# Four column groups in the second feed-forward product, one store, and w1 in three transfers of 112, 8 and 8 partitions

## The chip, the cores and the metric

The kernel runs on one core of a Trainium2 chip. The metric is the device time of one execution in microseconds (us); the kernel before takes 87.88 us, the median of three runs from 87.72 to 87.97. The profile shows one execution whose span, from the first to the last recorded instruction, is 86.1 us. Times inside the kernel are counted from the start of that span.

## What is computed

One decode step of a transformer block for four sequences (B = 4, one token each, width D = 512). A vector `c` is turned into six modulation vectors; then come attention over the last 1024 cached positions and a feed-forward layer with ReLU, each behind a layer norm that is scaled and shifted, and each added back through a gate:

```python
mod = (_silu(c) @ w_mod).reshape(c.shape[0], 6, 1, -1)
sa, ca, ga, sb, cb, gb = (mod[:, i] for i in range(6))
h = _layernorm(x) * (1 + ca) + sa
x = x + ga * attention(h, k_cache, v_cache, wq, wo)   # 32 heads, 8 key heads
h = _layernorm(x) * (1 + cb) + sb
x = x + gb * (relu(h @ w1) @ w2)                       # w1: 512 x 1792, w2: 1792 x 512
```

(The six slices are written as a loop here; the reference copies them one by one.) All inputs are bf16. Every weight and every cache entry is used once, so some 32 MB are read for very little arithmetic.

## The kernel before

All loads are issued by the SyncE queue (SP), in the order in which they are wanted: two key tiles, w_mod, wq in four parts, six more key tiles, eight value tiles, wo in four parts of 1 MB (`WO_CHUNKS`, L112 to 114), w1 as one transfer of 128 partitions (L119) and w2 in three transfers of 768, 768 and 256 KB (`W2_CHUNKS`, L123 to 125). The order of instructions on the other engines is the order of the program; each engine waits where its operands are not there yet.

Activations are kept transposed: features on the partitions, the four sequences along the free axis (`xT`, `xs2`, `h2T`). Three matmuls want the four sequences as the *stationary* operand: the gate `gb` (`gb_ps`, L227), the residual brought back to rows (`x12_ps`, L381) and the second feed-forward product (`z_ps`, L400). For these, `siluT32`, `xs2` and `uT32` are tiles with 32 columns (CG = 32), zero but for columns 0 to 3. A stationary operand of 32 columns fills a quarter of TensorE's columns, a column group. The kernel uses NH = 2 of the four groups: group 0 makes output columns 0 to 255 and writes to PSUM partitions 0 to 31, group 1 makes columns 256 to 511 and writes to partitions 32 to 63. So z_ps has 64 partitions, of which 0 to 3 and 32 to 35 carry results.

The end of the kernel, step by step: the last part of wo ends the attention product `y_ps` (L367: 128 matmuls, 32 for each part); VectorE adds the residual (L372, L373); `layernorm_T` (L242 to L261) takes two matmuls, six small VectorE operations and two ScalarE ones to make `h2T`; `ffn1` (L393) makes the hidden units in groups that follow W2_CHUNKS, 14 blocks of 128, each from four matmuls, and VectorE applies the ReLU (L395) into `uT32`; `ffn2` (L400) multiplies each block by its rows of w2 in two matmuls of 256 columns; VectorE multiplies by the gate (L410) and adds the residual (L412); two stores, one from SyncE and one from ScalarE, write the two halves of the rows (L414, L415).

```python
for (m0, m1) in U_GROUPS:
    ffn1(m0, m1)
for (m0, m1) in U_GROUPS:
    ffn2(m0, m1)
```

So TensorE does all of ffn1, then all of ffn2, and each group of ffn2 waits for its own transfer of w2.

Of the kernel before, what the change touches and what calls it, by code (L numbers as in the profile page):

```python
# [9 lines left out]
ALU = mybir.AluOpType  # L10
# [7 lines left out]
def kernel(  # L18
# [14 lines left out]
    nc = tc.nc  # L33
    P = 128
    B, Sq, D = A_x.shape
# [9 lines left out]
    CG = 32  # L45
# [7 lines left out]
    NI = W // KC  # L53
    RB = KC
    KAHEAD = 2
    NH = 2
    DH2 = D // NH

    ctx.enter_context(tc.manual_schedule(engines={
        mybir.EngineType.PE, mybir.EngineType.Activation, mybir.EngineType.DVE, mybir.EngineType.Pool}))  # L60
# [28 lines left out]
    wmod_sb = wts.tile([P, DT, 6 * D], bf16, tag="med", name="wmod_sb")  # L89
# [9 lines left out]
    for h in range(Hkv):  # L99
        vt_ = kvpool.tile([P, NI, Dh], bf16, tag="kv", name=f"v{h}")  # L100
        nc.sync.dma_start(
            out=vt_[:].rearrange("p j d -> p (j d)"),
            in_=A_v_cache[:, h, S - W:, :].rearrange("b (p j) d -> p b (j d)", j=NI),
# [5 lines left out]
    wo_sb = wts.tile([P, Hkv, NL, D], bf16, tag="big", name="wo_sb")  # L109
    wo_src = A_wo.rearrange("(h p l) n -> p h (l n)", h=Hkv, l=NL)  # L110
    wo_dst = wo_sb[:].rearrange("p h l n -> p h (l n)")
    WO_CHUNKS = [(0, 2), (2, 4), (4, 6), (6, 8)]  # L112
    for (h0, h1) in WO_CHUNKS:
        nc.sync.dma_start(out=wo_dst[:, h0:h1, :], in_=wo_src[:, h0:h1, :])

    w12 = wts.tile([P, DT * Dff + FT * D], bf16, tag="med", name="w12")
    w1_sb = w12[:, 0:DT * Dff].rearrange("p (t n) -> p t n", t=DT)
    w2_sb = w12[:, DT * Dff:DT * Dff + FT * D].rearrange("p (m n) -> p m n", m=FT)
    nc.sync.dma_start(out=w1_sb, in_=B_w1.rearrange("(t p) n -> p t n", p=P))  # L119
    FT2 = FT // 2  # L120
    w2_src = B_w2.rearrange("(m2 q e) n -> q m2 (e n)", q=P, e=2)
    w2_dst = w12[:, DT * Dff:DT * Dff + FT * D].rearrange("p (m2 en) -> p m2 en", m2=FT2)
    W2_CHUNKS = [(0, 3), (3, 6), (6, FT2)]  # L123
    for (m0, m1) in W2_CHUNKS:
        nc.sync.dma_start(out=w2_dst[:, m0:m1, :], in_=w2_src[:, m0:m1, :])  # L125

# [10 lines left out]
    siluT32 = const.tile([P, DT, CG], bf16, name="siluT32")  # L137
    nc.gpsimd.memset(siluT32[:], 0.0)
    ident_f = const.tile([P, P], f32, name="ident_f")
# [14 lines left out]
    uT32 = const.tile([P, FT, CG], bf16, name="uT32")  # L154
    nc.gpsimd.memset(uT32[:], 0.0)
    xs2 = const.tile([P, DT, CG], f32, name="xs2")
# [6 lines left out]
    cT = tp0[:, :, 0:B]  # L163
# [4 lines left out]
    f_c = work.tile([P, DT, B], f32, name="f_c")  # L168
# [2 lines left out]
    nc.vector.tensor_scalar_add(out=t_c[:], in0=t_c[:], scalar1=1.0)  # L171
    nc.vector.reciprocal(out=t_c[:], in_=t_c[:])
    nc.vector.tensor_tensor(out=f_c[:], in0=f_c[:], in1=t_c[:], op=ALU.mult)
    nc.vector.tensor_tensor(out=siluT32[:, :, 0:B], in0=cT, in1=f_c[:], op=ALU.mult)
    xT = work.tile([P, DT, B], f32, name="xT")
    nc.vector.tensor_copy(out=xT[:], in_=tp0[:, :, B:2 * B])

# [39 lines left out]
    mT = psA.tile([P, 5, DT, B], f32, tag="t", name="mT")  # L217
    for k in range(5):
        for m in range(DT):
            n0 = k * D + m * P  # L220
            for t in range(DT):
                nc.tensor.matmul(out=mT[:, k, m, :], lhsT=wmod_sb[:, t, n0:n0 + P], rhs=siluT32[:, t, 0:B],  # L222
                                 start=(t == 0), stop=(t == DT - 1))
    gb_ps = psA.tile([NH * CG, DH2], f32, tag="t", name="gb_ps")
    for t in range(DT):
        for nh in range(NH):
            nc.tensor.matmul(out=gb_ps[nh * CG:(nh + 1) * CG, :], lhsT=siluT32[:, t, :],  # L227
                             rhs=wmod_sb[:, t, 5 * D + nh * DH2:5 * D + (nh + 1) * DH2],
                             start=(t == 0), stop=(t == DT - 1), tile_position=(0, nh * CG))
    modT = work.tile([P, 5, DT, B], f32, name="modT")  # L230
    nc.vector.tensor_copy(out=modT[:], in_=mT[:])
    gb2 = work.tile([NH * CG, DH2], f32, name="gb2")
    nc.scalar.copy(out=gb2[:], in_=gb_ps[:])
# [35 lines left out]
    for t in range(DT):  # L269
        for hq in range(Hq):  # L270
            nc.tensor.matmul(out=qT_v[:, hq, :], lhsT=wq_sb[:, t, hq * Dh:(hq + 1) * Dh], rhs=hT[:, t, :],  # L271
                             start=(t == 0 and hq == 0), stop=(t == DT - 1 and hq == Hq - 1))
    for par in range(2):
        dst = qpad_s[:, :, par * NHW * CG:(par + 1) * NHW * CG].rearrange("p b (h c) -> p b h c", h=NHW)
        nc.vector.tensor_copy(  # L275
            out=dst[:, :, :, 16 * par:16 * par + rep],
            in_=qT_ps[:, par].rearrange("p h r b -> p b h r"))
# [35 lines left out]
    for iq in range(NQ):  # L313
        ws = slice(iq * WQ, (iq + 1) * WQ)
        nc.scalar.activation(out=e_sb[:, ws].rearrange("q (u k e) -> q u k e", k=KC, e=2),  # L315
                             in_=sc_ps[:, ws].rearrange("q (u e k) -> q u k e", e=2, k=KC), func=ACT.Exp,
                             bias=nb[:], scale=scale, accum_out=den4[:, iq:iq + 1])
    for iq in range(NQ):
        ws = slice(iq * WQ // 2, (iq + 1) * WQ // 2)
        nc.vector.tensor_tensor(out=p_w[:, ws, :], in0=e_w[:, ws].unsqueeze(2).to_broadcast([P, WQ // 2, B]),  # L320
                                in1=mi4[:].unsqueeze(1).to_broadcast([P, WQ // 2, B]), op=ALU.bitwise_and)
# [21 lines left out]
    for h in range(VEARLY, Hkv):  # L343
        pv(h, 0, NI, last=(h == Hkv - 1))
        if h == VEARLY:
# [6 lines left out]
                            in0=oT_ps[:].rearrange("p h a b r -> p (h a b r)"), in1=rb[:], op=ALU.mult)  # L352

    o4_ps = psA.tile([P, NL, NHW, 2, B], f32, tag="t", name="o4_ps")
    for l in range(NL):
        for r in range(rep):
            nc.tensor.matmul(out=o4_ps[r * RB:(r + 1) * RB, l], lhsT=ident_k3[:, l, :], rhs=oT_sb[:, :, :, :, r],
                             start=True, stop=True, tile_position=(0, r * RB))
# [5 lines left out]
    for h in range(Hkv):  # L364
        for l in range(NL):
            for m in range(DT):
                nc.tensor.matmul(out=y_ps[:, m, :], lhsT=wo_sb[:, h, l, m * P:(m + 1) * P], rhs=o4[:, l, h % NHW, h // NHW, :],  # L367
                                 start=(h == 0 and l == 0 and m == 0),
                                 stop=(h == Hkv - 1 and l == NL - 1 and m == DT - 1))
    yT = work.tile([P, DT, B], f32, name="yT")  # L370
    x1T = xs2[:, :, 0:B]
    nc.vector.tensor_tensor(out=yT[:], in0=y_ps[:], in1=ga, op=ALU.mult)  # L372
    nc.vector.tensor_tensor(out=x1T, in0=yT[:], in1=xT[:], op=ALU.add)  # L373

# [2 lines left out]

    x12_ps = psA.tile([NH * CG, DH2], f32, tag="t", name="x12_ps")
    for t in range(DT):
        nh, tl = t // 2, t % 2  # L380
        nc.tensor.matmul(out=x12_ps[nh * CG:(nh + 1) * CG, tl * P:(tl + 1) * P], lhsT=xs2[:, t, :], rhs=ident_f[:],  # L381
                         start=True, stop=True, tile_position=(0, nh * CG))


    w1_cols = [w1_sb[:, t, :].rearrange("p (m2 q e) -> p m2 e q", q=P, e=2) for t in range(DT)]
    z_ps = psA.tile([NH * CG, DH2], f32, tag="t", name="z_ps")
    U_GROUPS = [(2 * a, 2 * b_) for (a, b_) in W2_CHUNKS]

    def ffn1(m0, m1):
        u_ps = psA.tile([P, m1 - m0, B], f32, tag="t", name=f"u_ps_{m0}")  # L390
        for m in range(m0, m1):
            for t in range(DT):
                nc.tensor.matmul(out=u_ps[:, m - m0, :], lhsT=w1_cols[t][:, m // 2, m % 2, :], rhs=h2T[:, t, :],  # L393
                                 start=(t == 0), stop=(t == DT - 1))
        nc.vector.tensor_scalar_max(out=uT32[:, m0:m1, 0:B], in0=u_ps[:], scalar1=0.0)  # L395

    def ffn2(m0, m1):
        for m in range(m0, m1):
            for nh in range(NH):
                nc.tensor.matmul(out=z_ps[nh * CG:(nh + 1) * CG, :], lhsT=uT32[:, m, :],  # L400
                                 rhs=w2_sb[:, m, nh * DH2:(nh + 1) * DH2],
                                 start=(m == 0), stop=(m == FT - 1), tile_position=(0, nh * CG))

    for (m0, m1) in U_GROUPS:
        ffn1(m0, m1)
# [4 lines left out]
    nc.vector.tensor_tensor(out=zg[:], in0=z_ps[:], in1=gb2[:], op=ALU.mult)  # L410
    res = work.tile([NH * CG, DH2], bf16, name="res")
    nc.vector.tensor_tensor(out=res[:], in0=zg[:], in1=x12_ps[:], op=ALU.add)  # L412
    out_r = out.rearrange("b o d -> (b o) d")
    nc.sync.dma_start(out=out_r[:, 0:DH2], in_=res[0:B, :])  # L414
    nc.scalar.dma_start(out=out_r[:, DH2:D], in_=res[CG:CG + B, :])  # L415


# [28 lines left out]
```

## Time and profile before

| what | value |
|---|---|
| time, median of 3 | 87.88 us |
| span of the profiled execution | 86.1 us |
| TensorE matmul busy | 53.5 us, 62% of the span |
| VectorE, ScalarE busy | 23.7 us (28%), 22.8 us (26%) |
| read from memory | 31.99 MB, 373 GB/s mean over the span |
| transfers on the load queue | 90.8% of 16 engines' span |
| granted TensorE clock, mean | 0.713 |
| ffn1 matmuls (L393) | 56, from 77.5 us |
| ffn2 matmuls (L400) | 28, from 79.1 us, 418 ns each |
| the two stores issued | 83.64 and 83.65 us |

The share of busy time of the engines is a mean over stages. What sets the end is read from the chain that ended last: that is 69% transfers, 15% the SyncE queue's issuing and 10% TensorE. A matmul's duration is from its start to its end in a pipeline, so several can overlap, and the busy time of a group is less than the count times the duration.

### The profile page before, as it was taken

The page shows a single profiled execution, that of the slowest core. Times are in us where ns is not written, and L with a number is a line of the kernel's source. Part 1 is how long each engine was busy: PE and PEld are TensorE (multiplying, and loading weights), DVE is VectorE, ACT ScalarE, POOL GpSimd, SP SyncE. Part 2 cuts the span into 40 slices and gives each one's busy share as a digit, 9 for nine tenths or more (in the row PEclk, how much of TensorE's full clock was granted, in tenths as well). Part 3 has the DMA queues.
Part 4 walks back from the last instruction along what each step waited for, and adds up shares of the span by engine and source line. Part 5 has one row for each costly group of instructions (what it writes and reads, how often), then busy time and mean ns, then how long its engine had stood idle before and what let it go on. Part 6 is the DMA issues. An engine that isn't in the chain of part 4 may idle for free.

```text
span 86.1 us, 2373 instructions
## 1 busy us (share of the span) xinstructions
PE 53.5 (62%) x1074; PEld 45.0 (52%) x1074; DVE 23.7 (28%) x63; ACT 22.8 (26%) x35; POOL 3.5 (4%) x17
## 2 busy tenths in 40 slices
PE   0029920595393899999996099947354443379840
PEld 0029920574382379777881099937244443259510
DVE  0043470023200105765556695000020000432030
ACT  2314750001200026887773674010000000020000
POOL 6900000000000000000000000000000000000000
PEclk9999999755555557999999965975555555555555
DMA  0799999999999999999999999999999999999200
GB/s 2 329 415 412 414 425 425 428 426 415 426 426 423 415 423 419 415 411 423 426 407 419 419 426 426 430 407 411 411 402 411 413 396 410 399 389 353 101 0 2
DMA packets 6009, 32.14 MB, mean 373 GB/s; under 512 B 480, under 2 KB 496, under 8 KB 3440
## 3 DMA queue, kind: packets, MB, share of 16 engines
q1 hardware_dynamic: 5976, 31.99, 90.8%
q8 instruction: 8, 0.13, 0.6%
q10 hardware_dynamic: 24, 0.01, 0.1%
q14 instruction: 1, 0.01, 0.0%
HBM read 31.99 MB, written 0.00 MB: 372 GB/s over the span
## 4 chain that ended last, share of the span: by engine, by line
DMA 69%; SPq 15%; PE 10%; DVE 1%; issue 1%; DVEq 0%
DMA wq_sb<-in_A_wq_dram 27%; DMA v<-in_A_v_cache_dram 23%; DMA w<-in_B_w_dram 19%; SPq L119 5%; SPq L125 5%; PE ktp L187 5%; PE z_ps L400 2%; PE sc_ps L199 2%; SPq L94 2%; SPq L81 1%; PE qT_ps L271 1%; SPq L90 1%; DVE zg L410 0%; DVE res L412 0%; DVE qpad L275 0%
## 5 line engine op out<-in xcount | busy, mean ns | idle before, releaser
L192 ACT COPY kT<-ktp 128x1024 bf16<-128x1024 bf16 x16 | 15.5, 1015 | 15.2 <-PE ktp L187 14.1
L187 PEld LDWEIGHTS <-k 128*128 128x128 bf16 x256 | 17.1, 109 | 3.9 <-DMA k<-in_A_k_cache_dram 2.2
L187 PE MATMUL ktp<-ident_k,k 128*128 128x128 bf16 x256 | 18.1, 239 | 1.3 <-DMA k<-in_A_k_cache_dram 1.3
L190 DVE COPY kT<-ktp 128x1024 bf16<-128x1024 bf16 x16 | 11.1, 692 | 11.7 <-PE ktp L187 11.4
L309 PE MATMUL oT_ps<-pT,v 128*128 128x16 bf16 x256 | 7.5, 172 | 3.2 <-issue 1.7
L309 PEld LDWEIGHTS <-v 128*128 128x128 bf16 x256 | 7.2, 101 | 3.5 <-issue 1.8
L367 PE MATMUL y_ps<-o,wo_sb 128*128 128x4 bf16 x128 | 4.1, 167 | 5.3 <-DMA wo_sb<-in_A_wo_dram 5.3
L367 PEld LDWEIGHTS <-wo_sb 128*128 128x128 bf16 x128 | 3.7, 104 | 5.7 <-DMA wo_sb<-in_A_wo_dram 5.7
L255 ACT ACTIVATE lnv_ln<-var_ln,eps_t 128x4 f32<-128x4 f32 x2 | 0.6, 298 | 21.5 <-DVE var_ln L253 21.5
L271 PE MATMUL qT_ps<-hT,wq_sb 128*128 128x4 bf16 x128 | 3.9, 166 | 3.3 <-DMA wq_sb<-in_A_wq_dram 1.7
L199 PE MATMUL sc_ps<-kT,qpad 128*32 128x512 bf16 x64 | 5.6, 445 | 0.4 <-DVE qpad L275 0.4
L271 PEld LDWEIGHTS <-wq_sb 128*128 128x128 bf16 x128 | 3.7, 104 | 3.5 <-DMA wq_sb<-in_A_wq_dram 1.9
L222 PE MATMUL mT<-siluT,wmod_sb 128*128 128x4 bf16 x80 | 2.3, 166 | 4.7 <-DMA wmod_sb<-in_w_mod_dram 4.7
L326 PE MATMUL pT_ps<-ident_bf,p_rep 128*128 128x128 bf16 x32 | 3.1, 278 | 2.9 <-DVE p_rep L320 2.9
L222 PEld LDWEIGHTS <-wmod_sb 128*128 128x128 bf16 x80 | 2.2, 104 | 4.9 <-DMA wmod_sb<-in_w_mod_dram 4.9
L326 PEld LDWEIGHTS <-p_rep 128*128 128x128 bf16 x32 | 2.7, 127 | 3.4 <-DVE p_rep L320 3.4
L400 PE MATMUL z_ps<-w,uT 128*32 128x256 bf16 x28 | 3.4, 415 | 0.3 <-DMA w<-in_B_w_dram 0.3
L162 PE MATMUL tp<-ident_bf,cx_sb 8*128 8x8 bf16 x4 | 0.2, 163 | 4.6 <-DMA cx_sb<-in_A_x_dram 4.6
L351 DVE TENSOR_TENSOR oT_sb<-oT_ps,rb 128x128 bf16<-128x128 f32 x1 | 0.3, 292 | 9.4 <-PE oT_ps L309 9.4
L320 DVE TENSOR_TENSOR p_rep<-e_sb,mi 128x512 int32<-128x512 int32 x4 | 2.5, 688 | 0.7 <-ACT e_sb L315 0.7
L372 DVE TENSOR_TENSOR yT<-y_ps,modT 128x16 f32<-128x16 f32 x1 | 0.2, 174 | 9.1 <-PE y_ps L367 9.1
L400 PEld LDWEIGHTS <-uT 128*32 128x32 bf16 x28 | 2.0, 137 | 1.1 <-issue 0.6
(76 smaller groups left out, 35.3 us busy)
## 6 DMA issues: line engine op xcount, KB each, us to landing
k<-in_A_k_cache_dram SPq DMA_DIRECT2D x8, 1024.0 KB, 21.2
v<-in_A_v_cache_dram SPq DMA_DIRECT2D x8, 1024.0 KB, 19.8
wq_sb<-in_A_wq_dram SPq DMA_DIRECT2D x4, 1024.0 KB, 17.5
wo_sb<-in_A_wo_dram SPq DMA_DIRECT2D x4, 1024.0 KB, 20.1
wmod_sb<-in_w_mod_dram SPq DMA_DIRECT2D x1, 3072.0 KB, 14.0
w<-in_B_w_dram SPq DMA_DIRECT2D x1, 1792.0 KB, 22.2
w<-in_B_w_dram SPq DMA_DIRECT2D x2, 768.0 KB, 18.1
w<-in_B_w_dram SPq DMA_DIRECT2D x1, 256.0 KB, 13.7
```

The costliest lines, as they stand in the source:

```text
L119: nc.sync.dma_start(out=w1_sb, in_=B_w1.rearrange("(t p) n -> p t n", p=P))
L125: nc.sync.dma_start(out=w2_dst[:, m0:m1, :], in_=w2_src[:, m0:m1, :])
L187: nc.tensor.transpose(out=tp[:, ii, :], in_=k_tiles[gi][:, iq * IQ + ii, :], identity=ident_k)
L190: nc.vector.tensor_copy(out=dst, in_=tp[:])
L192: nc.scalar.copy(out=dst, in_=tp[:])
L199: nc.tensor.matmul(out=sc_ps[hw * CG:(hw + 1) * CG, half * HALF:(half + 1) * HALF], lhsT=qpad[:, b, par, hw, :], rhs=kT[:, half * (NI // 2 ...
L222: nc.tensor.matmul(out=mT[:, k, m, :], lhsT=wmod_sb[:, t, n0:n0 + P], rhs=siluT32[:, t, 0:B], start=(t == 0), stop=(t == DT - 1))
L271: nc.tensor.matmul(out=qT_v[:, hq, :], lhsT=wq_sb[:, t, hq * Dh:(hq + 1) * Dh], rhs=hT[:, t, :], start=(t == 0 and hq == 0), stop=(t == DT ...
L309: nc.tensor.matmul(out=oT_ps[:, hw, par].rearrange("p b r -> p (b r)"), lhsT=v_tiles[h][:, i, :], rhs=pT[:, i, c0:c0 + B * rep], start=(fi ...
L326: nc.tensor.transpose(out=tp[:, ii, :], in_=p_rep[:, i // 2, :, i % 2], identity=ident_bf[:])
L367: nc.tensor.matmul(out=y_ps[:, m, :], lhsT=wo_sb[:, h, l, m * P:(m + 1) * P], rhs=o4[:, l, h % NHW, h // NHW, :], start=(h == 0 and l == 0 ...
L400: nc.tensor.matmul(out=z_ps[nh * CG:(nh + 1) * CG, :], lhsT=uT32[:, m, :], rhs=w2_sb[:, m, nh * DH2:(nh + 1) * DH2], start=(m == 0), stop= ...
```

## The change

NH goes from 2 to 4, so the three products with a 32-column stationary operand use all four column groups, with 128 output columns for each. Within a group of 32 the four sequences now stand in every eighth column (BS = CG // B = 8) rather than in the first four. As 4 groups x 4 sequences then are 16 partitions spaced evenly by 8, one strided read of `res` holds the whole result, and one store replaces two. The writers and readers of siluT32, xs2 and uT32 take the stride.

The loads are cut differently. The last part of wo becomes two of 512 KB; w2's second transfer becomes two (512 and 256 KB), which also makes four groups of ffn1 and ffn2 out of three; w1 is loaded as partitions 0 to 111, 112 to 119 and 120 to 127. This gives the DMA engines uneven shares of w1, while the same bytes arrive in the same tile.

```diff
-    NH = 2
+    NH = 4
     DH2 = D // NH
+    BS = CG // B
...
-    WO_CHUNKS = [(0, 2), (2, 4), (4, 6), (6, 8)]
+    WO_CHUNKS = [(0, 2), (2, 4), (4, 6), (6, 7), (7, 8)]
...
-    nc.sync.dma_start(out=w1_sb, in_=B_w1.rearrange("(t p) n -> p t n", p=P))
+    w1_src = B_w1.rearrange("(t p) n -> p t n", p=P)
+    for (p0, p1) in [(0, 112), (112, 120), (120, 128)]:
+        nc.sync.dma_start(out=w1_sb[p0:p1], in_=w1_src[p0:p1])
...
-    W2_CHUNKS = [(0, 3), (3, 6), (6, FT2)]
+    W2_CHUNKS = [(0, 3), (3, 5), (5, 6), (6, FT2)]
...
-    nc.vector.tensor_tensor(out=siluT32[:, :, 0:B], in0=cT, in1=f_c[:], op=ALU.mult)
+    nc.vector.tensor_tensor(out=siluT32[:, :, ::BS], in0=cT, in1=f_c[:], op=ALU.mult)
...
-    x1T = xs2[:, :, 0:B]
+    x1T = xs2[:, :, ::BS]
...
-        nh, tl = t // 2, t % 2
-        nc.tensor.matmul(out=x12_ps[nh * CG:(nh + 1) * CG, tl * P:(tl + 1) * P], lhsT=xs2[:, t, :], rhs=ident_f[:],
-                         start=True, stop=True, tile_position=(0, nh * CG))
+        nc.tensor.matmul(out=x12_ps[t * CG:(t + 1) * CG, :], lhsT=xs2[:, t, :], rhs=ident_f[:],
+                         start=True, stop=True, tile_position=(0, t * CG))
...
-        nc.vector.tensor_scalar_max(out=uT32[:, m0:m1, 0:B], in0=u_ps[:], scalar1=0.0)
+        nc.vector.tensor_scalar_max(out=uT32[:, m0:m1, ::BS], in0=u_ps[:], scalar1=0.0)
...
-    out_r = out.rearrange("b o d -> (b o) d")
-    nc.sync.dma_start(out=out_r[:, 0:DH2], in_=res[0:B, :])
-    nc.scalar.dma_start(out=out_r[:, DH2:D], in_=res[CG:CG + B, :])
+    nc.sync.dma_start(out=out.rearrange("b o (g n) -> (o g) b n", g=NH), in_=res[::BS, :])
```

More of the change, by code (lines that the diff above doesn't have):

```diff
@@ L221 @@
             for t in range(DT):
-                nc.tensor.matmul(out=mT[:, k, m, :], lhsT=wmod_sb[:, t, n0:n0 + P], rhs=siluT32[:, t, 0:B],
+                nc.tensor.matmul(out=mT[:, k, m, :], lhsT=wmod_sb[:, t, n0:n0 + P], rhs=siluT32[:, t, ::BS],
                                  start=(t == 0), stop=(t == DT - 1))
```

## The prediction

> **What bounds the kernel now.** I read the busy slices first, then the chain of waits in order of time, the timeline of the last 14 us, and last the windows over the end of the stream. The slices (page part 2) and the queues (part 3):
>
> ```profile
> DMA  0799999999999999999999999999999999999200
> GB/s 2 329 415 412 414 425 425 428 426 415 426 426 423 415 423 419 415 411 423 426 407 419 419 426 426 430 407 411 411 402 411 413 396 410 399 389 353 101 0 2
> q1 hardware_dynamic: 5976, 31.99, 90.8%
> q8 instruction: 8, 0.13, 0.6%
> ```
>
> 32 MB stream in at some 400 GB/s from 2.6 us to about 81 us with no gap. Only two things can move the end: when the stream's last useful bytes land, and what runs after them. The 8 packets of q8 matter below: 0.6% of 16 engines x 86.1 us over 8 packets is 1.03 us each[...]. The end of the chain, in order of time (start, duration, what):
>
> ```profile
> 64.09 16.70 DMA w<-in_B_w_dram
> 80.78 0.04 issue
> 80.82 1.90 PE z_ps L400 x16
> 82.73 0.02 issue
> 82.75 0.43 DVE zg L410
> 83.18 0.02 issue
> 83.20 0.41 DVE res L412
> ```
>
> The second w2 transfer lands at 80.78, then come 16 matmuls, two VectorE operations and the store: 1.90, 0.43 and 0.41 us that nothing covers. The timeline says how much slack TensorE has ahead of that landing:
>
> ```profile
> 72.38 1.01 PE L367 MATMUL y_ps<-o,wo_sb 128*128 128x4 bf16 x32 [1.53 <-DMA wo_sb<-in_A_wo_dram]
> ...
> 77.51 1.63 PE L393 MATMUL u_ps<-h2T,w 128*128 128x4 bf16 x56 [0.55 <-DVE h2T L261]
> ...
> 79.07 1.47 PE L400 MATMUL z_ps<-w,uT 128*32 128x256 bf16 x12
> 80.82 1.89 PE L400 MATMUL z_ps<-w,uT 128*32 128x256 bf16 x16 [0.29 <-DMA w<-in_B_w_dram]
> ```
>
> TensorE waits 0.29 us for the landing. Data alone, made 0.6 us earlier, would gain only half of it; TensorE has to shorten too. The windows of the stream's end (last two columns: mean share of 16 DMA engines busy, GB/s):
>
> ```profile
> core 0: us, PE busy (x) PEld busy (x) DVE busy (x) ACT busy (x) POOL busy (x), PEclk, DMA share, GB/s
> 78.50:79.00 0.50, 0.50 (x24) 0.50 (x21) 0.04 (x2) 0.00 (x0) 0.00 (x0) 0.50 1.15 410
> 79.00:79.50 0.50, 0.50 (x12) 0.36 (x10) 0.31 (x2) 0.00 (x0) 0.00 (x0) 0.50 0.70 258
> 79.50:80.00 0.50, 0.50 (x8) 0.38 (x6) 0.00 (x0) 0.00 (x0) 0.00 (x0) 0.50 0.54 209
> 80.00:80.50 0.50, 0.50 (x6) 0.20 (x3) 0.00 (x0) 0.00 (x0) 0.00 (x0) 0.50 0.55 197
> 80.50:81.00 0.50, 0.21 (x5) 0.13 (x4) 0.00 (x0) 0.00 (x0) 0.00 (x0) 0.50 0.24 82
> ```
>
> From about 79.2 half of the DMA engines have finished; the other half runs on to 81, some 1.6 us more. A transfer lands when its slowest engine does, so the late half sets everything.
>
> [...] L199's 64 matmuls of 445 ns in four groups are busy for 5.6 us, not 28.
>
> **The change part by part.**
>
> *Four column groups (L400).* Today each of the 14 row blocks of w2 is a pair of 256-column matmuls run together. 16 take 1.89 us and 12 take 1.47, so a pair adds 0.21. Four 128-column matmuls together should add half, 0.107. One takes about 0.30 us (between L357's 196 ns at 32 columns and L400's 418 at 256). Four weight loads per 0.107 us rather than two per 0.21 are needed; L357 runs 16 such load and matmul pairs in 0.31 us, so loads allow it. The 28 extra instructions cost nothing beyond that.
>
> *w2 in four transfers (3, 2, 1, 1 of the 256 KB pieces).* The last piece takes 13.7 us from its issue to landing (part 6 of the page); the timeline has that issue start at 67.76, so it lands at 81.46, and its matmuls, last in order, are not held today. At 385 GB/s a piece is 0.68 us, so the new landings without any rebalancing are 78.8, 80.1, 80.8 and 81.46. Is TensorE ready for these? wo's last megabyte in two halves lets 16 of the 32 matmuls at 72.38 run earlier: 16 x 31.6 ns = 0.50 us off, so h2T comes at 76.86 rather than 77.36. w1 was issued at 54.70 and lands 22.2 us later, at 76.9, hence ffn1 runs 76.95 to 78.6, and the first six blocks (6 x 0.107) are done by 79.5. TensorE is now ahead of every later landing. After the last one: 0.04 to start, one more block 0.107, one matmul 0.30: z ends at 81.91, not 82.72. **-0.81 us.**
>
> *w1 as 112 + 8 + 8 partitions.* A partition of w1 is 4 x 3584 = 14,336 B, at 24.1 GB/s for an engine (385/16) 0.59 us. [...] the early half, some 1.6 us ahead, can take one more. **-0.59 us**; unknown cost, from -0.59 to the +0.59 and the port case below.
>
> *VectorE end (L410, L412).* 128 partitions x 128 elements instead of 64 x 256. L351, of that form, takes 0.29 us; 0.43 + 0.41 becomes 0.29 + 0.29: **-0.26 us.**
>
> *One store.* 16 rows of 256 B instead of two transfers of 4 rows of 512 B. The two are issued within 0.01 us of each other (83.64, 83.65), so removing ACT's gains nothing. Three more packets per engine: a packet of q10 averages 0.1% x 16 x 86.1 / 24 = 57 ns, so 0 to 0.17; I take **+0.10 us.**
>
> *What lies beside other work.* gb_ps (16 matmuls for 8) runs at 18.3, inside the wait for wq that ends at 27.35. The strided siluT feeds mT, same stretch. x_ps (1.08 us at 75.88) runs under the VectorE chain of the second layer norm and in four groups gets shorter. The strided x1T adds perhaps 0.02 us to each of five small steps, 0.1 us, inside TensorE's new lead. One extra ReLU (0.18 us) comes after the fourth group of u_ps and before a block that waits for data. Issues on the SP queue: the last landed 13.7 us after it began, so four more issues of 0.4 to 0.6 us delay no byte; only the store is queued behind them, at 83.6.
>
> Sum: -0.81 - 0.59 - 0.26 + 0.10 = -1.56, so 87.88 becomes 86.3 us.
>
> **The rivals.**
> - *Rebalancing does nothing*, because the engines get the same bytes or because one early engine is held too: -0.81 - 0.26 + 0.10 = -0.97, **86.9 us**. For it: share 0.54 is slightly over 8/16, so one more engine may be late.
> - *The wrong half.* [...] The last landing moves from 81.46 to 82.05: -0.81 + 0.59 - 0.26 + 0.10 = -0.38, **87.5 us**. No view names the engines. [...]
> - *Ports, the slower side.* [...] z then ends at 83.7, +0.98; with -0.26 + 0.10 that is +0.82, **88.7 us**. [...] Against it: engines, not ports, look limiting here, since half of the engines at 0.54 still move 24 GB/s each, as all 16 do. [...]
>
> **How the numbers follow.** Forecast (near 86.3) 0.49, no rebalancing 0.17, wrong half 0.15, ports 0.19. The range runs from 85.8 (store free, two more late engines caught up, 0.4 below) to 88.2, taking in wrong half and a mild port case; it leaves out the full port case and a small low tail. Faster by over 0.3% (below 87.62): the first two, and two thirds of the third, 0.76. Within 0.3%: 0.05. Slower: 0.19.
>
> **What would show it.** Right: z_ps in 56 matmuls with about 8 after the last landing, DVE's two operations at 0.29, the last bytes near 80.4, and the DMA share falling from 1 to 0 over less than 1 us. Wrong: half of the engines still busy from 79 to 81.5 (wrong half), a share near 0.5 during w1 with ffn1 waiting for w1 past 78 (ports), or z_ps blocks 0.2 us apart (the four groups do not run together).

## The result and the profile after

The changed kernel takes 95.17 us (median of 4, 94.70 to 95.59) against 87.80 before: ratio 1.0838, 95% interval 1.0780 to 1.0897. It is 7.4 us slower, where 86.3 us was forecast. Two of the four runs of `e2_split_only` and one of the eleven of `e7_spread`, each over 1.5% above the fastest of its kernel, are left out of the times below; the trace of `e7_spread` is of that one, whose span, 86.1 us, is like that of the others (86.1 to 86.4). The slices of the profiled execution (page part 2, span 92.9 us) show where:

```profile
DMA  1999999999999999999999999999999999999200
GB/s 37 351 388 419 418 431 432 430 409 427 413 423 413 430 416 420 416 427 416 413 423 420 423 416 420 411 406 406 411 409 279 226 239 157 134 259 362 103 2 2
```

Before, the rate stayed near 400 GB/s up to the last two slices of the stream. Now it falls to 226, then to 134, and recovers only from about 84 us on. The line above it hides this: the DMA engines count as busy throughout. The windows give it by stage, first of the changed kernel, then of the one before over three of the same stretches:

```profile
core 0: us, PE busy (x) PEld busy (x) DVE busy (x) ACT busy (x) POOL busy (x), PEclk, DMA share, GB/s
68.00:70.00 2.00, 0.50 (x19) 0.41 (x16) 0.00 (x0) 0.00 (x0) 0.00 (x0) 0.50 1.01 404
70.50:72.50 2.00, 0.90 (x28) 0.73 (x25) 0.00 (x0) 0.00 (x0) 0.00 (x0) 0.50 1.04 223
72.50:74.50 2.00, 0.59 (x16) 0.50 (x16) 0.00 (x1) 0.00 (x0) 0.00 (x0) 0.50 1.03 233
74.50:76.50 2.00, 0.61 (x3) 0.56 (x3) 0.89 (x5) 0.00 (x0) 0.00 (x0) 0.50 1.02 231
78.00:81.00 3.00, 0.00 (x0) 0.00 (x0) 0.38 (x3) 0.00 (x0) 0.00 (x0) 0.50 1.05 124
81.00:84.00 3.00, 0.00 (x0) 0.00 (x0) 0.00 (x0) 0.00 (x0) 0.00 (x0) 0.50 1.04 259
84.00:86.00 2.00, 1.00 (x38) 1.03 (x39) 0.19 (x1) 0.00 (x0) 0.00 (x0) 0.50 0.98 367
```

```profile
68.00:70.00 2.00, 0.47 (x18) 0.39 (x16) 0.00 (x0) 0.00 (x0) 0.00 (x0) 0.50 1.03 403
70.50:72.50 2.00, 0.47 (x17) 0.39 (x15) 0.00 (x0) 0.00 (x0) 0.00 (x0) 0.50 1.02 406
74.50:76.50 2.00, 1.22 (x9) 1.07 (x10) 0.70 (x4) 0.30 (x1) 0.00 (x0) 0.50 1.03 392
```

At 404 and 403 GB/s from 68 to 70 us, the two kernels are alike. w1's first packet is moved at 69.8 us. While its 112 partitions come in, the rate is 223 to 233; while the two transfers of 8 come in, 124. The share stays at 1 because each packet takes longer: in the trace's packet records the median 3584-byte packet of w1 takes 266 ns instead of 144, and the slowest 5% over 520. Against 400 GB/s I estimate from these rates that the stretches lose 7.5 us x (1 - 225/400) = 3.3 us, 3 x (1 - 124/400) = 2.1 and 3 x (1 - 259/400) = 1.1: 6.5 us of the 7.4. What TensorE sees of it, in the timeline after:

```profile
78.28 0.17 DVE L264 TENSOR_TENSOR h2T<-xc_ln,modT 128x16 bf16<-128x16 f32 x1
...
85.00 1.63 PE L394 MATMUL u_ps<-h2T,w 128*128 128x4 bf16 x56 [7.36 <-DMA w<-in_B_w_dram]
...
87.70 1.05 PE L401 MATMUL z_ps<-w,uT 128*32 128x128 bf16 x24 [0.31 <-DMA w<-in_B_w_dram]
...
88.98 0.41 PE L401 MATMUL z_ps<-w,uT 128*32 128x128 bf16 x8 [0.23 <-DMA w<-in_B_w_dram]
89.43 0.29 DVE L411 TENSOR_TENSOR zg<-z_ps,gb 128x128 f32<-128x128 f32 x1 [2.57 <-PE z_ps L401]
89.76 0.29 DVE L413 TENSOR_TENSOR res<-zg,x_ps 128x128 bf16<-128x128 f32 x1
90.07 0.67 SPq L414 DMA_DIRECT2D out_dram<-res  x1
```

h2T is written at 78.28, and ffn1 waits for w1 until 85.00; before, w1 was there first. The end itself is shorter, as intended: after the last landing 0.41 us of TensorE and two operations of 0.29.

### The profile page after: what moved, and what is told of

The parts are those of the page before. It is cut to its first block, busy times and chain, and to the rows that moved or that the text cites. A ratio compares the mean times of both kernels' runs of the same rounds, so it can differ in the third digit from the quotient of the medians.

```text
span 92.9 us, 2449 instructions
## 1 busy us (share of the span) xinstructions
PE 53.1 (57%) x1110; PEld 45.2 (49%) x1110; DVE 23.8 (26%) x64; ACT 22.8 (25%) x35; POOL 3.5 (4%) x17
## 4 chain that ended last, share of the span: by engine, by line
DMA 85%; PE 5%; SPq 4%; DVE 1%; issue 1%; DVEq 0%
DMA wq_sb<-in_A_wq_dram 24%; DMA v<-in_A_v_cache_dram 21%; DMA wo_sb<-in_A_wo_dram 21%; DMA w<-in_B_w_dram 19%; PE sc_ps L202 2%; PE ktp L190 2%; SPq L95 2%; SPq L82 1%; PE qT_ps L274 1%; SPq L91 1%; PE z_ps L401 0%; DVE zg L411 0%; DVE res L413 0%; DVE qpad L278 0%; DVEq L278 0%
## 5 line engine op out<-in xcount | busy, mean ns | idle before, releaser
L190 PEld LDWEIGHTS <-k 128*128 128x128 bf16 x256 | 18.2, 114 | 3.9 <-DMA k<-in_A_k_cache_dram 2.2
L190 PE MATMUL ktp<-ident_k,k 128*128 128x128 bf16 x256 | 19.3, 248 | 1.2 <-DMA k<-in_A_k_cache_dram 1.2
L394 PE MATMUL u_ps<-h2T,w 128*128 128x4 bf16 x56 | 1.6, 166 | 7.4 <-DMA w<-in_B_w_dram 7.4
L394 PEld LDWEIGHTS <-w 128*128 128x128 bf16 x56 | 1.6, 104 | 7.8 <-issue 7.8
L329 PEld LDWEIGHTS <-p_rep 128*128 128x128 bf16 x32 | 2.2, 111 | 3.6 <-DVE p_rep L323 3.4
L396 DVE TENSOR_SCALAR uT<-u_ps 128x8 bf16<-128x8 f32 (+2 forms) x4 | 0.9, 222 | 7.5 <-PE u_ps L394 7.5
```

The lines of the kernel that those rows point to most:

```text
L190: nc.tensor.transpose(out=tp[:, ii, :], in_=k_tiles[gi][:, iq * IQ + ii, :], identity=ident_k)
L329: nc.tensor.transpose(out=tp[:, ii, :], in_=p_rep[:, i // 2, :, i % 2], identity=ident_bf[:])
```

## Which part does it

The theory: the way w1 is cut slows its writes, because the rate of a transfer depends on which partitions it writes. The texts on record call this theory "ports", as they do the last rival of the prediction; what in the hardware would make the rate so, no run here shows. Rivals: another part of the change (column groups, strides, finer pieces, the store) does the harm; or some engines are simply given too much ("shares"); or a larger number of transfers, or small ones, are slow in themselves. As to the shares, the trace after has 16 landing events for the transfer of 112 partitions and 8 for each transfer of 8. I read them as one for each engine that a transfer uses; no trace numbers the engines.

**w1 whole, all else of the change** (`e1_whole`).

```diff
-    for (p0, p1) in [(0, 112), (112, 120), (120, 128)]:
+    for (p0, p1) in [(0, 128)]:
```

> The changed kernel with w1 as one transfer of 128 partitions; all else of the change stays. Cut theory (the loss comes from how w1 is cut): the loss goes and the other parts show their gain, about 86.9 us as in the prediction's sum without rebalancing (-0.81 - 0.26 + 0.10). Rival (the strides, the column groups, the finer w2 pieces or the single store do the harm): it stays above 90 us.

Measured 87.31 us, ratio to before 0.9946 (0.9933 to 0.9960). The loss is gone. The rate stays near 400 GB/s to the end of the stream, and TensorE ends at 81.88 us (the slices, then the last matmuls in the chain: start, duration, what):

```profile
GB/s 2 328 407 405 418 423 418 433 426 403 426 430 426 422 419 419 411 419 415 426 426 422 422 422 415 426 396 426 413 399 409 407 406 406 406 390 388 205 0 2
...
81.45 0.43 PE z_ps L401 x8
```

**The cut of w1 alone, in the kernel before** (`e2_split_only`).

```diff
-    nc.sync.dma_start(out=w1_sb, in_=B_w1.rearrange("(t p) n -> p t n", p=P))
+    w1_src = B_w1.rearrange("(t p) n -> p t n", p=P)
+    for (p0, p1) in [(0, 112), (112, 120), (120, 128)]:
+        nc.sync.dma_start(out=w1_sb[p0:p1], in_=w1_src[p0:p1])
```

> The kernel before with only w1 cut into 112, 8 and 8 partitions. Cut theory: the whole loss is here, 95 to 96.5 us. Rival (other parts do the harm): 87 to 88.5 us.

Measured 94.46 us (the mean of two runs, 93.80 and 95.11), ratio 1.0756 (1.0696 to 1.0815): these three lines alone lose 6.6 us. As all else of the change loses nothing without them, the other parts are ruled out as the cause. In the changed kernel the cut costs 7.9 us (95.17 against 87.31); why that is about 1 us more is open.

## Why the cut is slow

**Two transfers, 112 and 16** (`e3_112_16`).

```diff
-    for (p0, p1) in [(0, 112), (112, 120), (120, 128)]:
+    for (p0, p1) in [(0, 112), (112, 128)]:
```

> The changed kernel with w1 cut into 112 and 16 partitions. [...] Ports theory [...]: still slow, 112 partitions at the 220 GB/s seen in the changed kernel cost 3.1 us more than at 400, [...]: about 91.5 us. Shares theory [...]: the loss is gone, about 87 us.

Measured 93.81 us, ratio 1.0689 (1.0666 to 1.0711): 6.5 us over w1 whole, and far from the shares theory. Of the 4.6 us expected, 3.1 come from the rate measured in the changed kernel; the 1.5 for the 16 partitions was an estimate that no trace had shown. The shares are even as far as the page tells: it counts 541 packets under 512 B, one of them on q14 that the changed kernel has not, where w1 whole has 524. So the second transfer adds 16 of them, as many as a transfer of 128 partitions has landing events.

**Two transfers, two halves** (`e4_64_64`).

```diff
-    for (p0, p1) in [(0, 112), (112, 120), (120, 128)]:
+    for (p0, p1) in [(0, 64), (64, 128)]:
```

> The changed kernel with w1 cut into two halves of 64 partitions[...]. Ports theory: [...] about 90.8 us. Shares theory: no loss, about 87 us.

Measured 92.81 us, ratio 1.0586 (1.0549 to 1.0623), 5.5 us over w1 whole where 3.5 was expected, from a rate for 64 partitions that no trace had shown. Three of its windows while w1 arrives:

```profile
71.00:72.00 1.00, 0.43 (x16) 0.43 (x16) 0.00 (x0) 0.00 (x0) 0.00 (x0) 0.50 0.97 206
75.00:76.00 1.00, 0.58 (x2) 0.50 (x2) 0.24 (x2) 0.00 (x0) 0.00 (x0) 0.50 1.03 226
78.00:79.00 1.00, 0.00 (x0) 0.00 (x0) 0.52 (x3) 0.00 (x0) 0.00 (x0) 0.50 1.05 209
```

The 16 engines count as busy (a share of 0.97 to 1.07), and the rate is halved: over 71 to 82 us each window of 1 us shows 182 to 229 GB/s. The second transfer adds 16 packets under 512 B here too (540 against 524). The rates of the eleven windows add up to an estimated 2.35 MB, and w1 is 1.84 MB: some 0.5 MB of other transfers moves at the low rate as well.

With 112 partitions the rate is much the same, 223 to 233 GB/s (the changed kernel, 70.5 to 76.5 us). What sets it, for 64 or for 112, is not shown: no trace here says which partition a packet writes.

**Three transfers, all partitions** (`e5_by_rows`).

```diff
-    for (p0, p1) in [(0, 112), (112, 120), (120, 128)]:
-        nc.sync.dma_start(out=w1_sb[p0:p1], in_=w1_src[p0:p1])
+    for (t0, t1) in [(0, 2), (2, 3), (3, 4)]:
+        nc.sync.dma_start(out=w1_sb[:, t0:t1], in_=w1_src[:, t0:t1])
```

> The changed kernel with w1 still in three transfers, but cut along the free axis (two, one and one of the four 128-row blocks), so that each has all 128 partitions. Ports theory: no loss, 87.3 us, as with w1 whole. Rival (three transfers cost more than one): 88 us or more.

Measured 87.33 us, ratio 0.9946 (0.9931 to 0.9961). The number of transfers costs nothing; the axis of the cut does.

**The same bytes to near and to spread partitions** (`e6_near`, `e7_spread`). Both leave w1 whole and add two transfers of 8 rows into a tile that nothing reads; only the destination differs.

```diff
+    spare = wts.tile([P, DT, Dff], bf16, tag="spare", name="spare")
+    nc.sync.dma_start(out=spare[112:120], in_=w1_src[112:120])     # e7: spare[0:32:4]
+    nc.sync.dma_start(out=spare[120:128], in_=w1_src[120:128])     # e7: spare[1:32:4]
```

> The changed kernel with w1 whole, and after it two more transfers that read the same rows of w1 again (partitions 112 to 119 and 120 to 127, 115 KB each) into the same partitions of a spare tile that nothing reads. Ports theory: their packets, 8 for each of eight engines, take about 0.58 us as in the changed kernel instead of 0.14, 4.6 us; the early half of the engines has 1.6 us to spare, so about 87.3 + 3.0 = 90.3 us. Rival (a transfer of 8 partitions isn't slow in itself): 8 x 0.144 = 1.15 us on engines with 1.6 us to spare, 87.3 to 87.5 us.

> As the kernel with the two spare transfers, the same source rows and bytes, but written to partitions 0, 4, ... 28 and 1, 5, ... 29 of the spare tile[...]. Ports theory: packets back at 0.14 us; then 87.3 to 87.5 us [...]. Rivals (the small size, the number of engines or the source rows make such transfers slow): the same time as with the near partitions, about 90 us.

Measured: near 92.43 us, ratio 1.0529 (1.0503 to 1.0555); spread 88.01 us, ratio 1.0026 (1.0014 to 1.0038). The windows after w1, near first, then spread:

```profile
75.00:76.00 1.00, 1.00 (x10) 0.63 (x10) 0.17 (x1) 0.21 (x1) 0.00 (x0) 0.50 1.03 121
76.00:77.00 1.00, 0.12 (x4) 0.00 (x0) 0.52 (x3) 0.29 (x2) 0.00 (x0) 0.50 1.05 118
```

```profile
75.00:76.00 1.00, 1.00 (x10) 0.65 (x10) 0.17 (x1) 0.19 (x1) 0.00 (x0) 0.50 1.04 402
76.00:77.00 1.00, 0.15 (x4) 0.00 (x0) 0.52 (x3) 0.31 (x2) 0.00 (x0) 0.50 1.05 391
```

Same source rows, same bytes, same number of packets: only where they are written differs, and the whole core's rate is 121 against 402 GB/s. The 3584-byte packets of the spread form take 144 ns (at most 153), those of the near form up to 633. This settles destination against source, size and count. Why the near partitions are slow is not shown: no run wrote to other sets of eight. The near form costs 5.1 us over w1 whole, not the 3.0 that I expected: I had charged the eight engines alone, but other transfers are held as well. (The 0.58 us for a packet is high: in the changed kernel the 3584-byte packets from 78 to 81 us take 476 ns in the median, 644 at most.) From 75 to 77 us the 2048-byte packets of w2 take 302 ns in the median with the near form, 87 with the spread.

The spread form costs 0.7 us, over the 0 to 0.2 that I had set for the case that the eight engines of the spare transfers are all early; with all of them late, the 8 packets of 0.144 us more on each would cost 1.1 by my estimate. The landing events in its trace point to why (8 for a spare transfer, 16 for w1): of its first spare transfer, six engines land at 75.4 to 76.0 us and two at 77.1. Of w1 itself, seven of 16 land at 76.5 to 76.8 and nine at 74.9 to 75.5. So two of the seven late engines are among the eight that carry 8-partition transfers; the changed kernel and the near form show the same six and two. A transfer lands with its last engine: before, the second transfer of w2 has its 16 events from 78.96 to 80.78 us, and TensorE starts on it at 80.82. With more work on these eight the last landing of w2 comes at 82.19 us instead of 81.41 with w1 whole, even at the full rate: as long as two of the eight are late, rebalancing by this cut can't bring it forward. Seven of the eight instruction packets (q8; 1.02 to 1.11 us each before) are moved before w1 lands, as many as there are late engines; which engine moved each the trace does not say, so what makes the seven late is not shown.

## The parts that help

**The column groups without the finer pieces** (`e8_groups_only`), and **the finer pieces without the groups** (`e9_cuts_only`).

```diff
# e8: the kernel with w1 whole, and
-    WO_CHUNKS = [(0, 2), (2, 4), (4, 6), (6, 7), (7, 8)]
+    WO_CHUNKS = [(0, 2), (2, 4), (4, 6), (6, 8)]
-    W2_CHUNKS = [(0, 3), (3, 5), (5, 6), (6, FT2)]
+    W2_CHUNKS = [(0, 3), (3, 6), (6, FT2)]
# e9: the kernel before with the two removed lines of e8 in place of its own
```

> The kernel before with four column groups, strides and one store alone: wo, w1 and w2 cut as before. After the second w2 piece (80.78) 6 + 2 row blocks follow at 0.107 rather than 0.213 us, but the last piece at 81.46 now holds the last two blocks, as with the finer cuts: z ends about 81.9 in both. So by the landing theory the finer cuts add nothing and this gives 87.3 us, as the changed kernel with w1 whole. Rival (the finer cuts carry part of the gain): about 87.6 us.

> The kernel before with the finer cuts of wo and w2 alone (two column groups, two stores). TensorE has 0.5 us more lead; after the landing at 80.78 come 2 x 2 pairs of 0.213 us, but the third piece now lands at about 80.8 and the fourth at 81.46, followed by two pairs and 0.42: z ends near 82.1 instead of 82.7, 87.2 us. Rival (TensorE is as late as before): 87.8 us.

Measured: groups alone 87.05 us, ratio 0.9910 (0.9897 to 0.9924), the fastest here; pieces alone 87.50, ratio 0.9952 (0.9939 to 0.9966), a gain smaller than the 0.6 us expected. The timeline of the groups alone:

```profile
80.87 1.05 PE L401 MATMUL z_ps<-w,uT 128*32 128x128 bf16 x32 [0.91 <-DMA w<-in_B_w_dram]
81.96 0.29 DVE L411 TENSOR_TENSOR zg<-z_ps,gb 128x128 f32<-128x128 f32 x1 [2.53 <-PE z_ps L401]
82.29 0.29 DVE L413 TENSOR_TENSOR res<-zg,x_ps 128x128 bf16<-128x128 f32 x1
82.60 0.68 SPq L414 DMA_DIRECT2D out_dram<-res  x1
```

32 matmuls of 128 columns in 1.05 us do the work of 16 of 256 in 1.89. TensorE now waits 0.91 us for w2 rather than 0.29. With w1 whole and the finer pieces the first VectorE operation starts at 81.91, 0.05 earlier: with the groups, the finer pieces give next to nothing. In the kernel with pieces alone TensorE runs all 28 wide matmuls without a gap from 79.03 and ends at 82.2; it, and not the transfer, sets the end there. The expectation had the transfer set it, near 82.1; that is 0.1 of the 0.2 us that were missing, and the rest is not placed.

**Two stores instead of one** (`e10_two_stores`).

```diff
-    nc.sync.dma_start(out=out.rearrange("b o (g n) -> (o g) b n", g=NH), in_=res[::BS, :])
+    out_r = out.rearrange("b o (g n) -> (o g) b n", g=NH)
+    nc.sync.dma_start(out=out_r[0:2], in_=res[0:2 * CG:BS, :])
+    nc.scalar.dma_start(out=out_r[2:4], in_=res[2 * CG:4 * CG:BS, :])
```

> The changed kernel with w1 whole, and the 16 result rows stored by two transfers of 8 rows, one from SyncE and one from ScalarE. In the kernel with w1 whole the one store takes 0.69 us to issue, against 0.36 before. If the issue grows with the rows, two of 8 take about 0.5 each side by side: 87.1 us. Rival (the issue is off the path, or the number of transfers counts): 87.3 us or more.

Measured 87.41 us, ratio 0.9958 (0.9946 to 0.9971), no gain. The issue takes 0.66 us on SyncE and 0.61 on ScalarE with 8 rows, 0.61 to 0.69 with 16 in other runs, and 0.36 and 0.28 in the kernel before with 4 rows each, whose pattern has one dimension less. So the issue does not grow with the rows from 8 to 16; whether the extra dimension is what doubles it was not tried.

**The closing waits** (`e11_one_more`, `e12_same_count`). From the start of the store's issue to the end of the span are 2.79 us with w1 whole and 2.57 with the groups alone, for the same store.

```diff
# e11: in the kernel with the groups alone
-    WO_CHUNKS = [(0, 2), (2, 4), (4, 6), (6, 8)]
+    WO_CHUNKS = [(0, 1), (1, 2), (2, 4), (4, 6), (6, 8)]
# e12: in the kernel with w1 whole
-    WO_CHUNKS = [(0, 2), (2, 4), (4, 6), (6, 7), (7, 8)]
+    WO_CHUNKS = [(0, 3), (3, 7), (7, 8)]
```

> The kernel with the column groups alone (87.05 us), and wo's first piece cut in two, 50 us before the end: one transfer more in all. Closing theory: the transfers take eight completion semaphores in turn, and at the end SyncE waits for all of them in a fixed order, 0.06 us for each wait. With the groups alone the store has the semaphore that is waited for last, so the other waits are over by then; one transfer more moves the store to the third of six waits, and three waits come after it: +0.18, 87.2 us. Rival (a cut of an early load costs nothing): 87.05 us.

> The changed kernel with w1 whole (87.31 us), with wo in pieces of 3, 4 and 1 of its eight parts rather than 2, 2, 2, 1, 1: w2's four pieces and wo's short last piece stay, and the number of transfers is that of the kernel with the column groups alone. Closing theory: the store is waited for last again, 87.05 us. Rival (the finer pieces at the end cost the 0.25 us): 87.3 us.

Measured: 87.33 us, ratio 0.9938 (0.9918 to 0.9957), and 87.25 us, ratio 0.9933 (0.9914 to 0.9952). In the traces the stretch from the store's issue to the end is 2.73 and 2.58 us, which fits the theory (2.57 + 0.18 and 2.57). They also show the waits: SyncE's last ones come 0.06 us apart in the same order of semaphores in each run, and the wait for the store is the second of six with w1 whole, the third in e11, and the last with the groups alone and in e12. So the order of the closing waits is seen in the traces. The times alone don't settle it: e11 moved by 0.28 where 0.18 was expected, and e12's median by only 0.06 where 0.26 was, with runs from 87.08 to 87.32.

## Why the prediction was wrong, step by step

- **w1 as 112 + 8 + 8: -0.59 us forecast, +7.9 measured** (95.17 against 87.31 with w1 whole). This is the step that failed. It priced a partition at 0.59 us of its engine's time (14,336 B at 24.1 GB/s), a rate read from transfers of all 128 partitions, and let only the number of partitions for each engine count. The runs show that the rate depends on which partitions a transfer writes: the median packet of w1 took 266 ns instead of 144, and the core moved 223 to 233 GB/s while the 112 partitions came in, 124 while the eights did. The balancing was wrong as well: it took the late engines to be those that carry no transfer of 8, which no view had shown, and two of the seven are among the eight that do, so the "wrong half" rival was nearer to them. That a partition might cost more was priced only as a rival ("ports"), at 0.19.
- **The ports rival was right that the destination sets the rate, and was mis-sized: 88.7 us against 95.2.** Its 88.7 us was my estimate, from a rate for 8 neighbouring partitions that no trace of before shows, and it charged the two transfers of 8 alone. The large one is itself slowed for over 7 us, by the estimate above about 3.3 us; and while the small ones run, other transfers are slowed too (from 78 to 81 us the 2048-byte packets of w2 take 311 ns in the median, 86 over the whole run before). The argument against ports, that half of the engines at the end move 24 GB/s each, came from transfers of all 128 partitions and said nothing of other shapes. Of its sign, ffn1 waiting for w1 past 78 us came true; the share near 0.5 did not, for the share stayed near 1 while the rate halved.
- **Four column groups: right.** z was to end at 81.91 without rebalancing; with w1 whole it ends at 81.88 (82.72 before), 0.107 us a row block as worked out. The finer pieces, counted in the same step, were not needed for it: with the groups alone z ends at 81.92.
- **VectorE at 0.29 + 0.29: right**, to 0.01 us.
- **One store: +0.10 forecast, +0.37 measured** (2.79 us from its issue to the end, 2.42 before). I counted packets; most of the cost is the issue, 0.69 for 0.36 us, and the 16 packets take only 18 to 26 ns each in the trace after. The landing events put 0.30 of the 0.37 between the start of the issue and the store's landing; the rest comes after it, among the closing waits.
- **Work called hidden: right.** The layer norm with the strided x1T takes 4.11 us from yT to ffn1 against 4.09; the strided write of xs takes 0.19 us instead of 0.17. x_ps takes 0.66 us instead of 1.08.
- Sum without the cut of w1: 86.9 us forecast, 87.31 measured; the span is 0.72 us shorter (-0.84 - 0.26 + 0.37 = -0.73) where -0.97 was forecast, and the store explains that difference. The time fell by only 0.50; the other 0.2 us lies outside the span, and its cause is open.

## What to carry to other kernels

Cut a load along the free axis, and keep all 128 partitions in each transfer: here a cut into three cost nothing along one axis and 7.9 us along the other. Where the DMA engines are busy all the time, read their rate and not their share, for a slowed packet counts as busy (here a share of 1.05 at 124 GB/s). Where a few engines finish late, find out which before shifting work between them.

## What the runs showed that I had not expected

- While a transfer of 64 or 112 partitions comes in, the core moves 182 to 229 or 223 to 233 GB/s instead of some 400, with all 16 engines busy. No run shows why.
- Two transfers of 115 KB to 8 neighbouring partitions bring the whole core down to about 120 GB/s for 3 to 4 us, other transfers included; the same bytes to every fourth partition leave it at about 400.
- The store's issue costs 0.61 to 0.69 us on SyncE for 8 and for 16 rows, against 0.36 for 4 rows in the simpler pattern.
